# Block-causal attention with a maxout MLP on one core: transposes in two row tiles, a reordered opening, and V loaded as fp32 by SP and cast on GpSimd

## The chip, the cores and the metric

The program runs on one core of a Trainium2 chip. The metric is the device time of one execution in microseconds (us). The core has five engines with a queue each, served strictly in program order: PE (TensorE, matmuls and transposes), DVE (VectorE), ACT (ScalarE), POOL (GpSimd) and SP (SyncE, which here only issues DMAs). POOL and SP both issue DMAs, POOL's being able to change the data type on the way.

## What is computed

```python
def _attn_ref(q, k, v):                      # (8, 8, 576, 64) fp32 each
    scores = matmul(q, k.transpose(0, 1, 3, 2)) / sqrt(64)
    mask = (pos[:, None] // 64) >= (pos[None, :] // 64)     # blocks of 64
    attn = softmax(where(mask, scores, -1e9))
    return matmul(attn, v)
x = attn_out.transpose(0, 2, 1, 3).reshape(4608, 512)
g = maximum(x @ w1, x @ w2)                  # w1, w2: 512 x 1024
out = g @ w_out                              # w_out: 1024 x 512, out fp32
```

## The kernel before

The attention goes by 32 *pairs*: pair p is two heads of batch b = p // 4 (hp = p % 4 is the place of the pair in its batch). The MLP goes by 9 *spans* of 512 tokens, and its matmuls are dealt out as filler between the attention's.

Loads. `load_qk` (L84) reads q and k of a pair, each as one DMA on SP into a tile of 72 partitions (RPP = 8 rows of a head per partition). `cast_qk` (L95) turns each into bf16, on POOL for pairs 2 to 31. `load_v` (L105) reads one chunk of 128 rows of V for all 8 heads, five chunks a batch, with a DMA that POOL issues and that casts to bf16 straight into `vv` (per head 64 columns of V and one of ones). The weights come by POOL's DMAs too, 8 pieces of w1 and w2 and 2 of w_out (L117, L120). The loads after the opening stand in the list `pending` and are issued pair by pair on POOL (L331 to L335).

Opening (L124 to L139). SP issues the loads of pairs 0 to 2; POOL issues chunk 0 of V; DVE then runs constant memsets (ones column and tail of `vv`, L129 and L130, and tails of `kT` and `aT`); then the casts of pair 0 (DVE and ACT), chunks 1 to 4 of V on POOL, the casts of pair 1 on DVE, and the transposes of pair 0.

One pair (L322 to L342), in program order:

- `burst_a` (L261): scores of key chunks 0 and 1 into two PSUM tiles u0 and u1 of two banks each, both heads; the contraction has 64 rows, so the two heads use partitions 0 to 63 and 64 to 127. ACT takes the exponentials of u0 and u1 into `aT`, POOL clears the upper half of each diagonal block (`mask`, L251).
- `fill(11)`: up to 11 matmuls of the MLP.
- `burst_b` (L272): the same for chunks 2 to 4 (u2, u3), with the POOL memsets L279 and L280. u2 and u3 take the PSUM tiles of u0 and u1.
- loads and casts of later pairs.
- `av` (L283) for query tiles 0 and 1: 6 matmuls with `aT` as weights, then a reciprocal and a multiply on DVE.
- `transposes` (L218) of pair p + 1: 8 for q and 8 for k, each with 72 rows of weights and 72 columns of the identity, then a copy out of PSUM, q by DVE (L231), k by ACT (L233).
- `fill(5)`, `av` for query tiles 2, 3, 4 (24 matmuls), `fill(11)`.
- `x_out` (L308): 5 transposes of 128 x 128 and one DVE copy into `xT`, the input of the MLP.

`h_unit` (L156) has 8 matmuls of 512 columns for one eighth of w1 and w2, `y_unit` (L178) 8 for one output tile, copied out by ACT and stored by SP. `moe` (L193) yields False while the tokens of a span are not done, and `fill` then stops: during batch b there are 96 matmuls ready (64 during batch 1, none during batch 0), and they go at 27 a pair until none is left. What remains after pair 31, 224 matmuls, runs at the end. PSUM has four one-bank tiles (`ps_m`) for all but the scores.

Of the kernel before, what the change touches and what calls it, by code (L numbers as in the profile page):

```python
# [14 lines left out]
def kernel(  # L15
# [67 lines left out]

    def load_qk(p):  # L84
        b, hp = divmod(p, HP)
        raws[p] = []
        for nm, src in (("q", q), ("k", k)):
            t = raw.tile([P, 2, RPP * D], FP32, name=f"{nm}raw")
            nc.sync.dma_start(
                out=t[:NP],  # L90
                in_=src[b, 2 * hp:2 * hp + 2].rearrange("h (p t) d -> p h (t d)", t=RPP),
            )
            raws[p].append(t)

    def cast_qk(p, engines):  # L95
        qk_n[p] = []
        for nm, t, copy in zip("qk", raws.pop(p), engines):
            n = qkn.tile([P, RPP, 2, D], BF16, name=f"{nm}n")
            copy(  # L99
                out=n[:NP].rearrange("p t h d -> p h t d"),  # L100
                in_=t[:NP].rearrange("p h (t d) -> p h t d", d=D),
            )
            qk_n[p].append(n)
# [32 lines left out]
    cast_qk(0, (nc.vector.tensor_copy, nc.scalar.copy))  # L136
    for c in range(1, NCH):
        load_v(0, c)
    cast_qk(1, (nc.vector.tensor_copy, nc.vector.tensor_copy))  # L139

    def batch_loads(b):
        return [(lambda c=c: load_v(b, c)) for c in range(NCH)]

    pending = []
    for f in range(4):
        pending.append(lambda f=f: load_w(w1_sb, w1r, f * 256, 256))
        pending.append(lambda f=f: load_w(w2_sb, w2r, f * 256, 256))
    pending += batch_loads(1)
    pending += [lambda: load_wo(0, 4), lambda: load_wo(4, 4)]
    LOADS_AT = {0: 8, 1: 9}  # L150
# [42 lines left out]
    def moe():  # L193
        ny = SPAN // P
        for i in range(NSPAN):
            for f in range(NFF):
                while done_tokens[0] < (i + 1) * SPAN:
                    yield False
                for _ in h_unit(i, f):
                    yield True  # L200
# [16 lines left out]

    def transposes(p):  # L218
        b, hp = divmod(p, HP)
        tiles = []  # L220
        for nm, src in zip("qk", qk_n.pop(p)):
            pt = ps_m.tile([P, RPP, NP], BF16, name=f"ps_{nm}T", tag="m")
            for j in range(RPP):
                nc.tensor.transpose(  # L224
                    pt[:, j, :], src[:NP, j].rearrange("p h d -> p (h d)"), ident[:NP, :NP],
                )
            t = (qT_r if nm == "q" else kT_r)[p % NT]
            dst = t[:, :S].rearrange("q (p j) -> q p j", j=RPP)
            sv = pt.rearrange("q j p -> q p j")
            if nm == "q":  # L230
                nc.vector.tensor_copy(out=dst, in_=sv)  # L231
            else:
                nc.scalar.copy(out=dst, in_=sv)  # L233
# [17 lines left out]
    def mask(p, a0, n=1, step=0):  # L251
        a = aT_r[p % NA]
        if n == 1:
            nc.gpsimd.memset(a[BLK:, :, a0:a0 + BLK], 0.0)  # L254
        else:
            nc.gpsimd.memset(
                a[BLK:, :, a0:a0 + n * step].rearrange("p h (n s) -> p h n s", s=step)[:, :, :, :BLK],
                0.0,
            )
# [115 lines left out]
```

## Time and profile before

| | |
|---|---|
| median of 3 runs | 343.23 us (341.82 to 343.73) |
| the profiled execution | 338.89 us, span 337.1 us |
| PE busy | 292.4 us (87%) |
| PE weight loads busy | 157.5 us (47%) |
| DVE busy | 178.5 us (53%) |
| ACT busy | 138.8 us (41%) |
| POOL busy | 125.4 us (37%) |
| share of PE in the chain that ended last | 80% |

The profile is of one execution. Busy shares are means over stages that differ; the timeline, which lists instructions in order of time (equal neighbours merged, with their count, start and length), and the chain of waits, which is followed back from the last instruction, tell the stages apart. A matmul's length includes its way through the array, so the pace of a stream is read from start to start.

### The profile page before, as it was taken

The page shows a single profiled execution, that of the slowest core. Times are in us where ns is not written, and L with a number is a line of the kernel's source. Part 1 is how long each engine was busy: PE and PEld are TensorE (multiplying, and loading weights), DVE is VectorE, ACT ScalarE, POOL GpSimd, SP SyncE. Part 2 cuts the span into 40 slices and gives each one's busy share as a digit, 9 for nine tenths or more (in the row PEclk, how much of TensorE's full clock was granted, in tenths as well). Part 3 has the DMA queues.
Part 4 walks back from the last instruction along what each step waited for, and adds up shares of the span by engine and source line. Part 5 has one row for each costly group of instructions (what it writes and reads, how often), then busy time and mean ns, then how long its engine had stood idle before and what let it go on. Part 6 is the DMA issues. An engine that isn't in the chain of part 4 may idle for free.

```text
span 337.1 us, 7097 instructions
## 1 busy us (share of the span) xinstructions
PE 292.4 (87%) x2880; PEld 157.5 (47%) x2880; DVE 178.5 (53%) x353; ACT 138.8 (41%) x198; POOL 125.4 (37%) x244
## 2 busy tenths in 40 slices
PE   0065469996999999999999999999999998999995
PEld 0053245554555545555555555555555554444442
DVE  0242124775556655665666566656656665455440
ACT  2053434436545454545454545454554444101112
POOL 2329643554554345434543554355433300000000
PEclk9999999999999999999999999999999999999999
DMA  7899997674087559754875478548853000011013
GB/s 144 168 163 185 222 163 173 92 98 26 2 134 110 124 131 135 112 119 133 129 117 120 118 126 121 123 126 111 132 118 98 31 33 34 31 62 64 31 62 124
DMA packets 57984, 36.63 MB, mean 109 GB/s; under 512 B 39008, under 2 KB 44128, under 8 KB 57952
## 3 DMA queue, kind: packets, MB, share of 16 engines
q0 software_dynamic: 42784, 7.87, 31.5%
q1 hardware_dynamic: 15168, 28.32, 29.0%
q8 instruction: 22, 0.36, 0.5%
q14 instruction: 10, 0.08, 0.1%
HBM read 34.60 MB, written 9.44 MB: 131 GB/s over the span
## 4 chain that ended last, share of the span: by engine, by line
PE 80%; DMA 7%; issue 4%; DVE 3%; ACT 2%; POOL 2%; POOLq 0%; ACTq 0%
PE ps_h L165 37%; PE ps_y L183 18%; PE ps_o L295 10%; PE ps_s L241 7%; DMA w_sb<-in_moe_w_dram 4%; DMA vv<-in_v_dram 4%; PE ps_x L314 3%; PE ps_qT L224 2%; PE ps_kT L224 2%; ACT aT L247 2%; DVE xp L303 2%; POOL w_sb L118 1%; DVE rec L301 1%; DVE vv L130 0%; POOL qn L99 0%
## 5 line engine op out<-in xcount | busy, mean ns | idle before, releaser
L247 ACT ACTIVATE aT<-ps_s 128x1024 bf16<-128x1024 f32 (+1 forms) x128 | 99.2, 831 | 120.1 <-PE ps_s L241 119.1
L165 PE MATMUL ps_h<-xT,w_sb 128*128 128x512 bf16 x576 | 139.2, 381 | 0.0
L165 PEld LDWEIGHTS <-w_sb 128*128 128x128 bf16 x576 | 52.3, 98 | 60.7 <-issue 6.2
L172 DVE CAST h<-ps_h 128x512 bf16<-128x512 f32 x72 | 49.6, 689 | 43.9 <-PE ps_h L165 43.5
L183 PE MATMUL ps_y<-wo_sb,g 128*128 128x512 bf16 x288 | 70.6, 379 | 0.0
L174 DVE TENSOR_TENSOR g<-h,ps_h 128x512 bf16<-128x512 bf16 x72 | 49.5, 687 | 13.3 <-PE ps_h L165 12.1
L295 PE MATMUL ps_o<-vv,aT 128*128 128x65 bf16 x960 | 43.6, 200 | 7.8 <-POOL aT L254 6.9
L301 DVE RECIPROCAL rec<-ps_o 128x4 f32<-128x4 f32 x64 | 12.1, 190 | 66.8 <-PE ps_o L295 66.7
L295 PEld LDWEIGHTS <-aT 128*128 128x128 bf16 x960 | 37.8, 102 | 18.9 <-POOL aT L254 7.2
L254 POOL MEMSET aT<- 64x128 bf16 x64 | 12.7, 200 | 85.4 <-ACT aT L247 85.3
L241 PE MATMUL ps_s<-qT,kT 64*128 64x64 bf16 (+4 forms) x384 | 37.0, 296 | 6.2 <-ACT aT L247 5.5
L183 PEld LDWEIGHTS <-g 128*128 128x128 bf16 x288 | 26.9, 98 | 31.1 <-issue 1.3
L189 ACT COPY y<-ps_y 128x512 f32<-128x512 f32 x36 | 21.2, 588 | 48.0 <-PE ps_y L183 42.2
L108 POOL DMA_DIRECT2D vv<-in_v_dram x40 | 33.8, 852 | 11.8 <-DVE vv L129 11.0
L303 DVE TENSOR_TENSOR xp<-ps_o,rec 128x256 bf16<-128x256 f32 x64 | 31.4, 491 | 2.2
L99 POOL CAST qn<-qraw 72x1024 bf16<-72x1024 f32 x30 | 31.2, 1039 | 1.9
L99 POOL CAST kn<-kraw 72x1024 bf16<-72x1024 f32 x30 | 31.3, 1043 | 0.0
L224 PE MATMUL ps_qT<-ident,qn 72*128 72x72 bf16 x256 | 14.8, 205 | 18.0 <-DVE qn L99 18.0
L233 ACT COPY kT<-ps_kT 128x576 bf16<-128x576 bf16 x32 | 20.1, 628 | 22.0 <-PE ps_kT L224 21.9
L241 PEld LDWEIGHTS <-kT 64*128 64x128 bf16 x384 | 14.8, 97 | 30.6 <-issue 22.3
L279 POOL MEMSET aT<- 64x128 bf16 x32 | 6.4, 201 | 55.0 <-ACT aT L247 55.0
L314 PE MATMUL ps_x<-ident,xp 128*128 128x128 bf16 x160 | 17.4, 230 | 8.8 <-DVE xp L303 8.8
(24 smaller groups left out, 109.5 us busy)
## 6 DMA issues: line engine op xcount, KB each, us to landing
qraw<-in_q_dram SPq DMA_DIRECT2D x32, 288.0 KB
kraw<-in_k_dram SPq DMA_DIRECT2D x32, 288.0 KB
out_dram<-y SPq DMA_DIRECT2D x36, 256.0 KB
vv<-in_v_dram POOLq DMA_DIRECT2D x32, 128.0 KB, 5.8
w_sb<-in_moe_w_dram POOLq DMA_DIRECT2D x8, 256.0 KB, 8.1
wo_sb<-in_moe_w_out_dram POOLq DMA_DIRECT2D x2, 512.0 KB, 13.0
vv<-in_v_dram POOLq DMA_DIRECT2D x8, 64.0 KB, 3.3
```

The source lines that it names most:

```text
L99: copy(out=n[:NP].rearrange("p t h d -> p h t d"), in_=t[:NP].rearrange("p h (t d) -> p h t d", d=D),)
L108: nc.gpsimd.dma_start(out=vv[:rows, c, :, :D], in_=v[b, :, c * P:c * P + rows, :].rearrange("h p d -> p h d"),)
L165: nc.tensor.matmul(pt[:], w_sb[:, c, f * P:(f + 1) * P], xT[:, c, t0:t0 + SPAN], start=(c == 0), stop=(c == NDM - 1),)
L172: nc.vector.tensor_copy(out=h1[:], in_=pt[:])
L174: nc.vector.tensor_max(g[:, f, :], h1[:], pt[:])
L183: nc.tensor.matmul(py[:], g[:, f, s * P:(s + 1) * P], wo_sb[:, f, :], start=(f == 0), stop=(f == NFF - 1),)
L224: nc.tensor.transpose(pt[:, j, :], src[:NP, j].rearrange("p h d -> p (h d)"), ident[:NP, :NP],)
L241: nc.tensor.matmul(ps[:m, hh, col:col + w], kT[r, c * P:c * P + m], qT[r, q0:q0 + w], start=True, stop=True,)
L247: nc.scalar.activation(out=aT_r[p % NA][:m, :, a0:a0 + w], in_=ps[:m, :, :w], func=AF.Exp, scale=scale,)
L295: nc.tensor.matmul(po[:, gi, hh, :], a[:, hh, a0:a0 + P], vv[:, c, 2 * hp + hh, :], start=(mm == 0), stop=(mm == n_mm - 1),)
L303: nc.vector.tensor_mul(xp[:, :n], po[:, :, :, :D], rec[:, :n].to_broadcast([P, n, 2, D]))
L314: nc.tensor.transpose(pt[:, t, :], src.rearrange("p a d -> p (a d)"), ident[:])
```

## The change

- `transposes` and `x_out` work on halves of 64 partitions. q and k of a pair lie in one tile of 128 partitions (q on 0 to 63, k on 64 to 127, 9 rows of a head per partition), are cast by one instruction, and are transposed in 9 pairs of matmuls with 64 rows and 64 columns. `x_out` has 5 + 4 transposes of 64 rows into two PSUM tiles, and two copies.
- `load_v` is issued on SP into an fp32 tile `vraw` (4 buffers), and `cast_v` on POOL writes `vv`.
- The opening has another order; the weights' DMAs are all issued there, between POOL's casts; for the first four pairs both copies of the transposes and the masks are on DVE.
- The transposes of pair p + 1 go ahead of `burst_b(p)`; `x_out(p - 1)` is now the first step of pair p.
- `fill` spreads what is ready evenly over the pairs left in the batch, 2/5, 1/5 and the rest: 9, 4, 11 of 24 in batches 2 to 6; 6, 3, 7 of 16 in batch 1; 10, 5, 12 in batch 7.

```diff
-    RPP = 8
-    NP = S // RPP
+    NP = 64
+    RPP = S // NP
...
+    vraw = ctx.enter_context(tc.tile_pool(name="vraw", bufs=4))
...
     def load_qk(p):
         b, hp = divmod(p, HP)
-        raws[p] = []
-        for nm, src in (("q", q), ("k", k)):
-            t = raw.tile([P, 2, RPP * D], FP32, name=f"{nm}raw")
+        raws[p] = t = raw.tile([P, 2, RPP * D], FP32, name="raw")
+        for r, src in ((0, q), (NP, k)):
             nc.sync.dma_start(
-                out=t[:NP],
+                out=t[r:r + NP],
...
+    def cast_qk(p, copy):
+        t = raws.pop(p)
+        qk_n[p] = n = qkn.tile([P, RPP, 2, D], BF16, name="qkn")
...
     def load_v(b, c):
-        vv = vv_r[b % NV]
         rows = min(P, S - c * P)
-        nc.gpsimd.dma_start(
-            out=vv[:rows, c, :, :D],
+        v_raws[b, c] = t = vraw.tile([P, H, D], FP32, name="vraw")
+        nc.sync.dma_start(
+            out=t[:rows], in_=v[b, :, c * P:c * P + rows, :].rearrange("h p d -> p h d"),
         )
+
+    def cast_v(b, c, copy):
+        rows = min(P, S - c * P)
+        copy(out=vv_r[b % NV][:rows, c, :, :D], in_=v_raws.pop((b, c))[:rows])
...
-    for p in range(3):
-        load_qk(p)
-    load_v(0, 0)
+    dve, pool, act = nc.vector.tensor_copy, nc.gpsimd.tensor_copy, nc.scalar.copy
+    load_qk(0)
     make_identity(nc, ident)
...
+    load_v(0, 0)
+    load_qk(1)
+    load_v(0, 1)
+    load_v(0, 2)
+    load_qk(2)
+    load_v(0, 3)
+    load_qk(3)
+    load_v(0, 4)
+    cast_qk(0, dve)
+    cast_v(0, 0, pool)
+    cast_qk(1, pool)
+    cast_v(0, 1, pool)
+    load_w(0, 256)
+    cast_v(0, 2, pool)
+    load_w(256, 256)
+    cast_qk(2, pool)
+    cast_v(0, 3, pool)
+    cast_v(0, 4, pool)
+    load_w(512, 256)
+    cast_qk(3, pool)
+    load_w(768, 256)
+    load_wo(0, 4)
+    load_wo(4, 4)
...
     def transposes(p):
+        n = qk_n.pop(p)
+        pq = ps_m.tile([P, RPP, NP], BF16, name="ps_qT", tag="m")
+        pk = ps_m.tile([P, RPP, NP], BF16, name="ps_kT", tag="m")
+        for j in range(RPP):
+            for r, pt in ((0, pq), (NP, pk)):
+                nc.tensor.transpose(
+                    pt[:, j, :], n[r:r + NP, j].rearrange("p h d -> p (h d)"),
+                    ident[r:r + NP, r:r + NP],
+                )
         tiles = []
+        for pt, ring_, copy in ((pq, qT_r, dve), (pk, kT_r, dve if p < HP else act)):
...
+    def mask(p, a0):
+        eng = nc.vector if p < HP else nc.gpsimd
+        eng.memset(aT_r[p % NA][BLK:, :, a0:a0 + BLK], 0.0)
...
+        pe = ps_m.tile([P, NCH, BLK], BF16, name="ps_xe", tag="m")
+        po = ps_m.tile([P, NCH - 1, BLK], BF16, name="ps_xo", tag="m")
         for t in range(NCH):
-            nc.tensor.transpose(pt[:, t, :], src.rearrange("p a d -> p (a d)"), ident[:])
+            src = (x01[:, t] if t < 2 else x234[:, t - 2]).rearrange("p a d -> p (a d)")
+            nc.tensor.transpose(pe[:, t, :], src[:BLK], ident[:BLK, :BLK])
+            if t < NCH - 1:
+                nc.tensor.transpose(po[:, t, :], src[BLK:], ident[BLK:, BLK:])
...
     for p in range(NPAIR):
         b, hp = divmod(p, HP)
+        if p > 0:
+            x_out(p - 1)
         burst_a(p)
-        fill(11)
-        burst_b(p)
-        if p + 3 < NPAIR:
-            load_qk(p + 3)
-        if p + 2 < NPAIR:
-            cast_qk(p + 2, (nc.gpsimd.tensor_copy, nc.gpsimd.tensor_copy))
...
-        av(p, [0, 1])
+        n = -(-ready() // (HP - hp)) if p < NPAIR - HP else 27
+        fill(n * 2 // 5)
         if p + 1 < NPAIR:
             transposes(p + 1)
-        fill(5)
+        burst_b(p)
+        if p + 4 < NPAIR:
+            load_qk(p + 4)
+        if 4 <= p + 2 < NPAIR:
+            cast_qk(p + 2, pool)
+        if b + 1 < B:
+            for c in range(hp * 2, min(hp * 2 + 2, NCH)):
+                load_v(b + 1, c)
+            if hp > 0:
+                for c in range(hp * 2 - 2, min(hp * 2, NCH)):
+                    cast_v(b + 1, c, pool)
+        av(p, [0, 1])
+        fill(n // 5)
         av(p, [2, 3, 4])
-        fill(11)
-        x_out(p)
-    while next(moe_steps, None) is not None:
-        pass
+        fill(n - n * 2 // 5 - n // 5)
+    x_out(NPAIR - 1)
+    fill(len(needs))
```

## Rows read from the trace of the kernel before

**Rows 1.** The page: GB/s moved in 40 equal slices of the span.
```profile
GB/s 144 168 163 185 222 163 173 92 98 26 2 134 110 124 131 135 112 119 133 129 117 120 118 126 121 123 126 111 132 118 98 31 33 34 31 62 64 31 62 124
```

**Rows 2.** Timeline, opening: start us, length us, engine, line, operation, count [idle before, releaser].
```profile
1.27 1.02 POOL L108 DMA_DIRECT2D vv<-in_v_dram  x1 [0.81 <-POOLq L359]
...
6.18 1.04 ACT L99 CAST kn<-kraw 72x1024 bf16<-72x1024 f32 x1 [4.15 <-DMA kraw<-in_k_dram]
13.44 0.09 DVE L129 MEMSET vv<- 128x40 bf16 x1 [13.44 <-DMA vv<-in_v_dram]
...
17.35 1.22 DVE L99 CAST qn<-qraw 72x1024 bf16<-72x1024 f32 x2
...
19.90 1.03 PE L241 MATMUL ps_s<-qT,kT 64*128 64x512 bf16 x6 [0.73 <-ACT kT L233]
...
23.99 1.51 PE L295 MATMUL ps_o<-vv,aT 128*128 128x65 bf16 x24
...
25.84 5.96 POOL L118 DMA_DIRECT2D w_sb<-in_moe_w_dram  x8
...
26.82 1.04 PE L241 MATMUL ps_s<-qT,kT 64*128 64x512 bf16 x6
...
31.84 0.34 POOL L254 MEMSET aT<- 64x128 bf16 x2
```

**Rows 3.** The chain that ended last: start us, length us, engine, line, count.
```profile
54.76 0.97 PE ps_s L241 x6
55.73 3.51 PE ps_h L165 x11
...
86.09 0.54 PE ps_s L241 x6
...
251.85 0.54 PE ps_s L241 x6
...
284.82 1.79 PE ps_h L165 x8
```

**Rows 4.** Timeline of one pair in the middle, 103.3 to 112.3 us.
```profile
103.40 0.61 PE L241 MATMUL ps_s<-qT,kT 64*128 64x512 bf16 x6
...
106.42 0.42 PE L241 MATMUL ps_s<-qT,kT 64*128 64x320 bf16 x6
...
106.78 0.36 PE L295 MATMUL ps_o<-vv,aT 128*128 128x65 bf16 x6
106.92 1.18 ACT L247 ACTIVATE aT<-ps_s 128x1024 bf16<-128x1024 f32 x2
...
106.97 0.42 PE L224 MATMUL ps_qT<-ident,qn 72*128 72x72 bf16 x8
...
107.49 1.25 PE L165 MATMUL ps_h<-xT,w_sb 128*128 128x512 bf16 x5
107.73 0.75 DVE L231 COPY qT<-ps_qT 128x576 bf16<-128x576 bf16 x1
107.99 0.62 ACT L233 COPY kT<-ps_kT 128x576 bf16<-128x576 bf16 x1
108.00 0.20 POOL L279 MEMSET aT<- 64x128 bf16 x1 [1.91 <-ACT aT L247]
...
108.67 0.88 PE L295 MATMUL ps_o<-vv,aT 128*128 128x65 bf16 x24
...
109.39 2.32 PE L165 MATMUL ps_h<-xT,w_sb 128*128 128x512 bf16 x10
...
111.76 0.44 PE L314 MATMUL ps_x<-ident,xp 128*128 128x128 bf16 x5
...
112.14 0.39 PE L241 MATMUL ps_s<-qT,kT 64*128 64x512 bf16 x2
```

**Rows 5.** Timeline of PE, a batch's last pair into the next batch, 152 us.
```profile
152.00 0.34 PE L314 MATMUL ps_x<-ident,xp 128*128 128x128 bf16 x3 [0.77 <-DVE xp L303]
```

**Rows 6.** Groups by line and shape: busy us, mean ns of one | idle before.
```profile
L99 POOL CAST kn<-kraw 72x1024 bf16<-72x1024 f32 x30 | 31.3, 1043 | 0.0
```

More of the change, by code (lines that the diff above doesn't have):

```diff
@@ L73 @@
     aT_r = [ring.tile([P, 2, AW + APAD], BF16, name=f"aT{r}") for r in range(NA)]
-    xT = ring.tile([P, NDM, NTOK], BF16, name="xT")
+    xT = ring.tile([P, NDM, NTOK + BLK], BF16, name="xT")
     w1_sb = wpool.tile([P, NDM, d_ff], BF16, name="w1_sb")
@@ L85, in load_qk @@
         b, hp = divmod(p, HP)
-        raws[p] = []
-        for nm, src in (("q", q), ("k", k)):
-            t = raw.tile([P, 2, RPP * D], FP32, name=f"{nm}raw")
+        raws[p] = t = raw.tile([P, 2, RPP * D], FP32, name="raw")
+        for r, src in ((0, q), (NP, k)):
             nc.sync.dma_start(
-                out=t[:NP],
+                out=t[r:r + NP],
                 in_=src[b, 2 * hp:2 * hp + 2].rearrange("h (p t) d -> p h (t d)", t=RPP),
             )
[L93 to L103, printed above, removed]
+    def cast_qk(p, copy):
+        t = raws.pop(p)
+        qk_n[p] = n = qkn.tile([P, RPP, 2, D], BF16, name="qkn")
+        copy(
+            out=n.rearrange("p t h d -> p t h d"),
+            in_=t.rearrange("p h (t d) -> p t h d", d=D),
+        )
+    v_raws = {}
     def load_v(b, c):
-        vv = vv_r[b % NV]
         rows = min(P, S - c * P)
-        nc.gpsimd.dma_start(
-            out=vv[:rows, c, :, :D],
-            in_=v[b, :, c * P:c * P + rows, :].rearrange("h p d -> p h d"),
-        )
+        v_raws[b, c] = t = vraw.tile([P, H, D], FP32, name="vraw")
+        nc.sync.dma_start(
+            out=t[:rows], in_=v[b, :, c * P:c * P + rows, :].rearrange("h p d -> p h d"),
+        )
+    def cast_v(b, c, copy):
+        rows = min(P, S - c * P)
+        copy(out=vv_r[b % NV][:rows, c, :, :D], in_=v_raws.pop((b, c))[:rows])
     w1r = moe_w1.rearrange("(c p) f -> p c f", p=P)
@@ L115, with load_w @@
     wor = moe_w_out.rearrange("(c p) f -> p c f", p=P)
-    def load_w(dst, src, f0, fw):
-        nc.gpsimd.dma_start(out=dst[:, :, f0:f0 + fw], in_=src[:, :, f0:f0 + fw])
+    def load_w(f0, fw):
+        for dst, src in ((w1_sb, w1r), (w2_sb, w2r)):
+            nc.gpsimd.dma_start(out=dst[:, :, f0:f0 + fw], in_=src[:, :, f0:f0 + fw])
     def load_wo(c0, n):
         nc.gpsimd.dma_start(out=wo_sb[:, c0:c0 + n, :], in_=wor[:, c0:c0 + n, :])
-    for p in range(3):
-        load_qk(p)
-    load_v(0, 0)
+    dve, pool, act = nc.vector.tensor_copy, nc.gpsimd.tensor_copy, nc.scalar.copy
+    load_qk(0)
     make_identity(nc, ident)
@@ L135 @@
         nc.vector.memset(aT_r[r][:BLK, :, AW:], 0.0)
[L136 to L150, printed above, removed]
+    load_v(0, 0)
[21 more added lines that the diff above has]
+    load_wo(4, 4)
     done_tokens = [0]
@@ L195, in moe @@
         for i in range(NSPAN):
+            need = (i + 1) * SPAN
             for f in range(NFF):
[L197 to L200, printed above, removed]
+                yield from ((need, 0) for _ in h_unit(i, f))
                 if i > 0 and f % 2 == 0:
-                    for _ in y_unit(i - 1, f // 2):
-                        yield True
+                    yield from ((need, 0) for _ in y_unit(i - 1, f // 2))
@@ L204, in moe, with ready @@
         for s in range(ny):
-            for _ in y_unit(NSPAN - 1, s):
-                yield True
-    moe_steps = moe()
+            yield from ((NTOK, 0) for _ in y_unit(NSPAN - 1, s))
+    needs = []
+    for i in range(NSPAN):
+        needs += [(i + 1) * SPAN] * (2 * NDM * NFF + (SPAN // P * NFF if i else 0))
+    needs += [NTOK] * (SPAN // P * NFF)
+    moe_steps = moe()
+    at = [0]
+    def ready():
+        n = at[0]
+        while n < len(needs) and needs[n] <= done_tokens[0]:
+            n += 1
+        return n - at[0]
@@ L210, in fill @@
     def fill(n):
-        for _ in range(n):
-            if not next(moe_steps, False):
-                return
+        for _ in range(min(n, ready())):
+            next(moe_steps)
+            at[0] += 1
     st = {}
     def transposes(p):
-        b, hp = divmod(p, HP)
-        tiles = []
[L221 to L233, printed above, removed]
+        n = qk_n.pop(p)
@@ new lines, in transposes @@
+        pq = ps_m.tile([P, RPP, NP], BF16, name="ps_qT", tag="m")
[5 more added lines that the diff above has]
+                    ident[r:r + NP, r:r + NP],
+                )
+        tiles = []
+        for pt, ring_, copy in ((pq, qT_r, dve), (pk, kT_r, dve if p < HP else act)):
+            t = ring_[p % NT]
+            copy(
+                out=t[:, :S].rearrange("q (p j) -> q p j", j=RPP),
+                in_=pt.rearrange("q j p -> q p j"),
+            )
@@ L249, in exp @@
         )
[L251 to L259, printed above, removed]
+    def mask(p, a0):
+        eng = nc.vector if p < HP else nc.gpsimd
+        eng.memset(aT_r[p % NA][BLK:, :, a0:a0 + BLK], 0.0)
     def burst_a(p):
@@ L278, in burst_b @@
         exp(p, u2, 512, 1024)
-        nc.gpsimd.memset(aT_r[p % NA][BLK:, :, 1024:1088], 0.0)
-        nc.gpsimd.memset(aT_r[p % NA][BLK:, :, 1344:1408], 0.0)
+        mask(p, 1024)
+        mask(p, 1344)
         exp(p, u3, 64, 1536, m=BLK)
@@ L310, in x_out @@
         _, _, x01, x234 = st.pop(p)
-        pt = ps_m.tile([P, NCH, P], BF16, name="ps_x", tag="m")
+        pe = ps_m.tile([P, NCH, BLK], BF16, name="ps_xe", tag="m")
+        po = ps_m.tile([P, NCH - 1, BLK], BF16, name="ps_xo", tag="m")
         for t in range(NCH):
-            src = x01[:, t] if t < 2 else x234[:, t - 2]
-            nc.tensor.transpose(pt[:, t, :], src.rearrange("p a d -> p (a d)"), ident[:])
-        px = pt.rearrange("p t w -> p (t w)")[:, :S]
-        nc.vector.tensor_copy(out=xT[:, hp, b * S:(b + 1) * S], in_=px)
+            src = (x01[:, t] if t < 2 else x234[:, t - 2]).rearrange("p a d -> p (a d)")
+            nc.tensor.transpose(pe[:, t, :], src[:BLK], ident[:BLK, :BLK])
+            if t < NCH - 1:
+                nc.tensor.transpose(po[:, t, :], src[BLK:], ident[BLK:, BLK:])
+        dst = xT[:, hp, b * S:b * S + NCH * P].rearrange("p (t h w) -> p t h w", h=2, w=BLK)
+        nc.vector.tensor_copy(out=dst[:, :, 0], in_=pe[:])
+        nc.vector.tensor_copy(out=dst[:, :NCH - 1, 1], in_=po[:])
         if hp == HP - 1:
```

5 lines of the change are left out of this document (removed).

## The prediction

> **What bounds the kernel now.** I read the chain of waits first. It is PE's own work for 80%, and it falls into stages [rows 3]: batch 0 ends when pair 4's first scores start at 54.76, batch 1 at 86.09, batch 7 starts at 251.85 and the remaining 224 MLP matmuls at 284.82. From 86.09 to 251.85 are 20 pairs, 8.29 us each.
>
> One pair of the middle, from the timeline, then says what a pair costs PE [rows 4]. The 11 matmuls of a fill take 109.39 to 111.76, 0.2155 each. Both score bursts, with the changes between array shapes around them, take 0.36 (106.42 to 106.78) and 106.42 - 103.40 - 11 x 0.2155 = 0.65. The small `av` takes 0.19, the 16 transposes 0.52 (32.5 ns each), the large `av` 0.72, `x_out` with the change behind it 0.38. Ahead of the large `av` lies 0.10 (107.49 + 5 x 0.2155 = 108.57, start 108.67): it starts as the copy of kT ends (108.61), whose PSUM tile it seems to take. With the 24 matmuls that a pair has on average this sums to 8.09. A batch's last pair runs out of filler, and `x_out` waits 0.77 for DVE [rows 5], 0.19 a pair: 8.28, against 8.29 found. So the sum of rows is the stage; ACT and DVE only matter where PE waits on them.
>
> The opening is another matter [rows 2]. DVE's first memset waits until 13.44 for the first V load, because both write `vv`; DVE casts only at 17.35, and the first scores start at 19.90. Pair 0 takes 6.92 (to 26.82). Four such pairs would end at 47.6, not 54.76: the masks of pair 1, ready for ACT's results long before, sit behind 5.96 us of weight DMA issues on POOL and run at 31.84.
>
> **The change, part by part.**
>
> *Transposes.* 16 of 32.5 ns become 9 pairs. No row has tiled transposes. Lower end: the scores run two heads on the two halves, and the second burst's 2 x 576 columns fit in 0.36 with a change of shape, where one after the other they need 1152 x 0.2155 / 512 = 0.48; so the halves do overlap, and 64 columns cost 64/512 x 0.2155 = 27 ns, as `av` with 65 columns and its own weights has 30. That gives 9 x 0.03 = 0.27. Upper end: no overlap, 18 x 0.0325 = 0.59. I take 0.27, since scores are the nearest thing. `x_out` goes from 5 x 0.054 to 5 x 0.03: 0.38 becomes 0.26 (upper end 0.40). No change of shape is added, as each group now stands beside a burst. The second DVE copy lies beside the scores.
> [...]
>
> *Transposes moved ahead of burst_b.* This is what gives the gain back. ACT is served in order, so it now has the copy of kT(p + 1) ahead of the exponentials of u2. Let T be the start of the transposes. Their results are there at T + 0.45 (eight end 0.42 after their start, a ninth adds 0.03); the copy starts at T + 0.48 and takes 0.62, the next ACT instruction starts 0.1 before its end as 107.99 against 106.92 + 1.18 shows: exponentials at T + 1.0, the first mask 1.08 later (106.92 to 108.00), 0.20 long: T + 2.28 [rows 4]. PE arrives at the large `av` at T + 0.27 + 0.36 + 0.19 + 4 x 0.2155 = T + 1.68. So **a wait of 0.60 a pair** takes the place of 0.10. Ends: 0, if ACT gets to the exponentials of u2 before the copy matters (then T + 1.68 covers it); 0.9, if POOL is 0.3 late with the mask, the length of a quarter of a q-k cast ahead of it.
>
> *Middle, batches 2 to 6.* 0.26 + 0.65 + 9 x 0.2155 + 0.27 + 0.36 + 0.19 + 0.86 + 0.60 + 0.72 + 11 x 0.2155 = 8.22 a pair, with nothing left of the 0.19. Against 8.29 that is 1.4 us in 20 pairs: almost nothing.
>
> *Batch 7.* With 27 a pair the wait shrinks to 0.38 and a pair takes 8.65; the last, with 15 and an exposed multiply as before, about 7.3: 33.2 against 284.82 - 251.85 = 33.0, so +0.2. The 224 matmuls behind it and the store stay.
>
> *Batch 1.* 16 a pair: 8.22 - 8 x 0.2155 + 0.22 (a step less of cover) = 6.71, times 4 = 26.8. PE starts it at half pace: 11 matmuls took 3.51 where 2.37 is usual, and the scores 0.97 for 0.54 [rows 3], so +1.5: 28.3 against 31.3. **-3.0.**
>
> *Opening.* DVE's memsets no longer wait; they take 3.9 (13.44 to 17.35). The last of k arrived by 6.18 [rows 2]. Cast, transposes at half pace and now two DVE copies of 0.75 [rows 4]: scores of pair 0 by about 9.2. But the large `av` of pair 0 needs chunk 4 of V, the last of 13 SP loads: 8 x 0.295 + 4.5 x 0.262 = 3.54 MB. At 222 GB/s, the highest slice [rows 1], that is there at 17.2; with the 2.1 MB of weights that POOL may request before it, at 163, near 36. I take 3.54 MB at 168 from 1.3 us on, 22.4, as the weights are issued between POOL's casts, which themselves wait for these loads. POOL casts 512 columns in 0.5 (1043 ns for 1024 [rows 6]): 22.9. Then six `av` matmuls at half pace, 0.4, and 1.3 to pair 1's scores (23.99 + 1.51 to 26.82 [rows 2]): 24.6. Three more pairs: 6.92, plus at most one more copy on DVE (0.75); I take 7.2, since the masks are now on DVE and wait for no DMA issue. Pair 4 starts at 46.2 instead of 54.76: **-8.6** (ends: 38.0 with V no limit, -16.8; 59.7, +4.9).
>
> *POOL and SP.* POOL loses 40 V issues and gains 40 casts of 0.5; q and k become one cast of 1152 columns, 1.2 for 2.1. In the middle the casts end well ahead of the next pair's masks. SP gains the V loads behind `out` stores, with a pair of time to spare. Nothing, as long as V lands within a pair.
>
> Sum: -8.6 - 3.0 - 1.4 + 0.2 = -12.8. The profiled execution's 338.9 becomes 326.1. It lies 4.3 under the median of the runs, so the median 343.2 becomes **330.4 us**.
>
> **The rivals.**
>
> *A, more is gained.* V is not the limit of the opening (pair 4 at 40) and the wait is half: 330.4 - 6 - 24 x 0.3 = 317. For: the V loads' 13.44 was queueing, and SP's ring gets chunk 4 no weights ahead. Against: 3.54 MB need time.
>
> *B, the halves don't overlap.* 0.32 a pair on the transposes and 0.14 on `x_out`, 28 pairs: +12.9, 343, no change. [...]
>
> *C, slower.* Batch 1 stays at the lower clock. [...] If it doesn't rise there, batch 1's 5.9 us of PE work a pair becomes 11.8: 4 x 5.1 - 1.5 = +19, **349 us**. [...]
>
> *D, the opening's gain goes.* Chunk 4 of V arrives behind the weights, pair 4 at 59.7: 330.4 + 13.5 = 344, no change. The same comes if SP takes long over V's 1024 short runs a chunk.
>
> **How the numbers follow.** Forecast 0.50, A 0.20, B 0.13, D 0.07, C 0.10. A measurement here can tell about 0.5% (341.5 to 344.9). Forecast, A and a little of B (tiles that overlap in part) are faster: 0.76; the rest of B and D are the same: 0.13; C and a worse wait: 0.11. The range 317 to 342 leaves out A's lower half and C, and holds most of B.
>
> **What would show it.** Right: DVE's first memset before 2 us; pair 4 at 46 with pair 0's large `av` waiting for the last cast of V; 30 ns from pair to pair of tiled transposes; ACT's kT copy ahead of the u2 exponentials, and 0.6 us of PE idle ahead of L295 on POOL's mask; pairs of 8.2 in the middle. Wrong: transposes at 60 ns a pair (B), 0.43 us matmuls beyond pair 4 (C), no idle ahead of L295 (A), or pair 4 after 50 us (D).

## The result, and the profile of the changed kernel

The changed kernel takes **330.5 us** (median of 4 runs, 328.75 to 331.5) against 342.52 (4 runs, 340.61 to 343.73): ratio 0.9648, 95% interval 0.9583 to 0.9714. The forecast was 330.4. The total is right, but several of its terms are not, and that they add up to it is chance.

The page of the changed kernel: span, GB/s in 40 slices, busy time, and the chain that ended last by engine.

```profile
span 329.7 us, 7518 instructions
...
GB/s 162 213 217 200 200 212 211 184 152 67 126 161 108 123 167 166 109 117 161 171 114 82 197 164 119 103 169 162 122 42 34 34 34 33 63 35 65 32 66 127
...
PE 283.3 (86%) x3072; PEld 146.2 (44%) x3072; DVE 184.7 (56%) x403; ACT 136.4 (41%) x193; POOL 86.9 (26%) x199
...
PE 48%; issue 23%; ACT 9%; DMA 8%; POOL 6%; SPq 4%; DVE 1%; POOLq 0%; ACTq 0%; DVEq 0%
```

PE's share of the chain was 80% and is 48%; ACT went from 2 to 9%, POOL from 2 to 6%, "issue" (time in which the engine waited for nothing that the profile shows) from 4 to 23%, and SP's own issues are new in it with 4%. The first seven slices move 162 to 217 GB/s where they moved 144 to 222 [rows 1], so the opening is full of transfers in both. Where each stage starts (each pair's first scores in the timeline) tells more than the total. `before` was profiled a second time; that execution took 343.54 us, near the median, where the first took 338.89:

| stage start, us | pair 1 | pair 4 | pair 8 | pair 28 | span |
|---|---|---|---|---|---|
| before, first profile | 26.82 | 54.69 | 86.02 | 251.78 | 337.1 |
| before, second profile | 26.74 | 55.77 | 89.37 | 256.41 | 341.8 |
| after | 23.80 | 44.33 | 78.18 | 244.46 | 329.7 |

| stage, us | forecast | after less first profile | after less second profile |
|---|---|---|---|
| opening, to pair 4 | -8.6 | -10.4 | -11.4 |
| batch 1, pairs 4 to 7 | -3.0 | +2.5 | +0.3 |
| batches 2 to 6 | -1.4 | +0.5 | -0.8 |
| the rest | +0.2 | -0.1 | -0.2 |
| sum | -12.8 | -7.4 | -12.1 |

The opening gave more than forecast, batch 1 nothing. The two profiles of `before` differ by 4.7 us, 3.4 of it up to pair 8 (89.37 against 86.02) and nearly all the rest in pair 8, where none had been expected. Their windows (length, busy of PE, PEld, DVE, ACT, POOL, granted clock, DMA share, GB/s) from 76 us on, the first profile's:

```profile
76.00:90.00 14.00, 10.34 (x165) 6.42 (x164) 7.61 (x17) 7.91 (x12) 6.38 (x14) 1.00 0.27 15
```

and the second's:

```profile
76.00:90.00 14.00, 10.54 (x144) 6.88 (x142) 7.59 (x17) 7.33 (x10) 6.18 (x14) 0.83 0.46 44
```

In the second the mean granted clock of that stretch is 0.83 where the first has 1.00, 144 matmuls stand in it in place of 165, and pair 8 took 9.91 us for 8.65. Pairs 2, 4 and 7 took 1.0 to 1.2 us more as well. The sum was built on an execution without that; the 4.3 us added to reach the median allowed for it as a whole, but no term of batch 1 did.

The opening of the changed kernel (timeline, columns as in [rows 2]):

```profile
0.96 0.09 DVE L131 MEMSET vv<- 128x40 bf16 x1 [0.96 <-PEq L379]
...
6.18 1.35 DVE L97 CAST qkn<-raw 128x1152 bf16<-128x1152 f32 x1 [1.23 <-DMA raw<-in_k_dram]
...
9.77 1.04 PE L260 MATMUL ps_s<-qT,kT 64*128 64x512 bf16 x6 [1.51 <-DVE kT L249]
...
17.33 7.53 SPq L89 DMA_DIRECT2D raw<-in_q_dram  x1
...
21.66 0.61 POOL L113 CAST vv<-vraw 64x512 bf16<-64x512 f32 x1 [4.22 <-DMA vraw<-in_v_dram]
...
23.80 1.09 PE L260 MATMUL ps_s<-qT,kT 64*128 64x512 bf16 x6
```

DVE's memset starts at 0.96 instead of 13.44, and the first scores at 9.77 instead of 19.90; but pair 0's large `av` waits for the cast of V's chunk 4, which ends at 22.27, and pair 1 starts at 23.80, 3.0 us sooner and not 10. The other 7.3 us come from pairs 1 to 3, 20.5 us instead of 27.9. They are not V's: in the runs e and k below, with V by the old path and without V, pairs 1 to 3 take the same 20.5. That the masks are now on DVE and no longer behind POOL's DMA issues [rows 2] is the likely cause; it was not tried alone. One SP issue is held for 7.53 us.

A pair of the middle:

```profile
105.72 0.20 PE L242 MATMUL ps_qT<-ident,qkn 64*128 64x64 bf16 x1
105.73 0.20 PE L242 MATMUL ps_kT<-ident,qkn 64*128 64x64 bf16 x1
105.76 0.19 PE L242 MATMUL ps_qT<-ident,qkn 64*128 64x64 bf16 x1
...
105.99 0.41 PE L260 MATMUL ps_s<-qT,kT 64*128 64x320 bf16 x6
106.28 0.64 ACT L249 COPY kT<-ps_kT 128x576 bf16<-128x576 bf16 x1 [0.71 <-PE ps_kT L242]
...
106.82 1.18 ACT L266 ACTIVATE aT<-ps_s 128x1024 bf16<-128x1024 f32 x2
...
107.40 0.22 PE L308 MATMUL ps_o<-vv,aT 128*128 128x65 bf16 x2
107.90 0.34 POOL L272 MEMSET aT<- 64x128 bf16 x2 [2.08 <-ACT aT L266]
108.16 0.84 PE L308 MATMUL ps_o<-vv,aT 128*128 128x65 bf16 x22 [0.54 <-POOL aT L272]
```

The nine pairs of transposes take 0.27 (105.72 to 105.99), where 16 took 0.52 [rows 4]. ACT now copies kT before it takes the exponentials of u2 (106.28, 106.82); the mask on them follows at 107.90, and the large `av`, begun at 107.40, gets its third matmul at 108.16, where 30 ns apart is usual: some 0.70 us of wait a pair.

Batch 1's first pair, rows of POOL and of PE:

```profile
47.50 0.62 POOL L113 CAST vv<-vraw 128x512 bf16<-128x512 f32 x1 [6.02 <-DMA vraw<-in_v_dram]
48.06 1.15 POOL L97 CAST qkn<-raw 128x1152 bf16<-128x1152 f32 x1
49.26 0.20 PE L242 MATMUL ps_qT<-ident,qkn 64*128 64x64 bf16 x1 [1.44 <-POOL qkn L97]
...
50.69 0.61 POOL L113 CAST vv<-vraw 64x512 bf16<-64x512 f32 x1 [1.49 <-DMA vraw<-in_v_dram]
51.36 0.63 POOL L272 MEMSET aT<- 64x128 bf16 x4
51.61 0.51 PE L308 MATMUL ps_o<-vv,aT 128*128 128x65 bf16 x6 [1.67 <-POOL aT L272]
...
54.53 3.18 PE L175 MATMUL ps_h<-xT,w_sb 128*128 128x512 bf16 x7
```

and the same stretch in windows (columns as above):

```profile
44.00:48.00 4.00, 3.59 (x17) 1.22 (x17) 1.38 (x4) 1.94 (x2) 0.50 (x1) 1.00 1.14 225
48.00:52.00 4.00, 1.07 (x31) 0.86 (x32) 0.76 (x1) 1.72 (x3) 2.45 (x7) 0.85 1.08 221
52.00:56.00 4.00, 4.00 (x34) 2.30 (x32) 2.04 (x5) 0.00 (x0) 1.14 (x1) 0.50 1.26 204
```

POOL waits 6.02 us for a chunk of batch 1's V, casts q and k of pair 5, for whose transposes PE stands idle 1.44 us, waits 1.49 for another chunk, and only then clears pair 4's diagonal blocks; PE's `av` waits 1.67 for that. PE is busy for 1.07 of 4 us, and the granted clock is at 0.50 in the next window; seven matmuls of `h` from 54.53 on take 3.18, 0.43 apart. Pair 4 lasts 13.44 us (10.27 before; the forecast comes to 8.2).

### The profile page after: what moved, and what is told of

Read it like the earlier page. It is cut to its first block, busy times and chain, and to the rows that moved or that the text cites. A ratio compares the mean times of both kernels' runs of the same rounds, so it can differ in the third digit from the quotient of the medians.

```text
span 329.7 us, 7518 instructions
## 1 busy us (share of the span) xinstructions
PE 283.3 (86%) x3072; PEld 146.2 (44%) x3072; DVE 184.7 (56%) x403; ACT 136.4 (41%) x193; POOL 86.9 (26%) x199
## 4 chain that ended last, share of the span: by engine, by line
PE 48%; issue 23%; ACT 9%; DMA 8%; POOL 6%; SPq 4%; DVE 1%; POOLq 0%; ACTq 0%; DVEq 0%
PE ps_h L175 25%; PE ps_y L193 11%; ACT aT L266 9%; PE ps_o L308 7%; DMA vraw<-in_v_dram 5%; DMA raw<-in_k_dram 4%; SPq L89 3%; POOL aT L272 3%; PE ps_s L260 2%; PE ps_xe L328 2%; POOL qkn L97 1%; POOL w_sb L121 1%; POOL vv L113 1%; ACT y L199 0%; SPq L107 0%
## 5 line engine op out<-in xcount | busy, mean ns | idle before, releaser
L182 DVE CAST h<-ps_h 128x512 bf16<-128x512 f32 x72 | 49.7, 690 | 47.6 <-PE ps_h L175 47.4
L193 PE MATMUL ps_y<-wo_sb,g 128*128 128x512 bf16 x288 | 74.7, 379 | 0.0
L308 PE MATMUL ps_o<-vv,aT 128*128 128x65 bf16 x960 | 48.5, 201 | 26.3 <-POOL aT L272 15.5
L314 DVE RECIPROCAL rec<-ps_o 128x4 f32<-128x4 f32 x64 | 11.8, 185 | 52.8 <-PE ps_o L308 52.7
L97 POOL CAST qkn<-raw 128x1152 bf16<-128x1152 f32 x31 | 35.5, 1147 | 4.1 <-DMA raw<-in_k_dram 2.4
L113 POOL CAST vv<-vraw 128x512 bf16<-128x512 f32 (+1 forms) x40 | 23.9, 617 | 28.6 <-DMA vraw<-in_v_dram 28.5
L249 DVE COPY qT<-ps_qT 128x576 bf16<-128x576 bf16 x32 | 24.1, 752 | 5.2 <-PE ps_kT L242 4.7
L249 ACT COPY kT<-ps_kT 128x576 bf16<-128x576 bf16 x28 | 17.9, 639 | 18.6 <-PE ps_kT L242 18.3
L242 PE MATMUL ps_qT<-ident,qkn 64*128 64x64 bf16 x288 | 15.0, 199 | 9.8 <-DVE qkn L97 7.6
L260 PEld LDWEIGHTS <-kT 64*128 64x128 bf16 x384 | 17.8, 99 | 10.0 <-issue 4.2
L242 PEld LDWEIGHTS <-qkn 64*128 64x128 bf16 x576 | 11.9, 100 | 22.4 <-issue 8.1
L242 PE MATMUL ps_kT<-ident,qkn 64*128 64x64 bf16 x288 | 15.1, 199 | 0.0
```

The lines of the kernel that those rows point to most:

```text
L97: copy(out=n.rearrange("p t h d -> p t h d"), in_=t.rearrange("p h (t d) -> p t h d", d=D),)
L193: nc.tensor.matmul(py[:], g[:, f, s * P:(s + 1) * P], wo_sb[:, f, :], start=(f == 0), stop=(f == NFF - 1),)
L242: nc.tensor.transpose(pt[:, j, :], n[r:r + NP, j].rearrange("p h d -> p (h d)"), ident[r:r + NP, r:r + NP],)
L249: copy(out=t[:, :S].rearrange("q (p j) -> q p j", j=RPP), in_=pt.rearrange("q j p -> q p j"),)
L260: nc.tensor.matmul(ps[:m, hh, col:col + w], kT[r, c * P:c * P + m], qT[r, q0:q0 + w], start=True, stop=True,)
L308: nc.tensor.matmul(po[:, gi, hh, :], a[:, hh, a0:a0 + P], vv[:, c, 2 * hp + hh, :], start=(mm == 0), stop=(mm == n_mm - 1),)
```

## The experiments

Three things were open: what the middle pair's wait is, what holds pair 4, and what sets the opening. "Pair" is the mean of pairs 8 to 27, (start of pair 28 - start of pair 8) / 20; it is 8.29 before and 8.31 after.

**a_fill.** The wait, tried by more filler behind the small `av`: 7, 7, 10 for 9, 4, 11.

```diff
-        fill(n * 2 // 5)
+        n1 = (n * 3 + 5) // 10
+        fill(n1)
...
-        fill(n // 5)
+        fill(n1)
...
-        fill(n - n * 2 // 5 - n // 5)
+        fill(n - 2 * n1)
```

> The changed kernel with the filler dealt out 3/10, 3/10, 4/10 of a pair (7, 7, 10 of 24) in place of 9, 4, 11; nothing else moves. Theory (PE waits 0.7 us a pair ahead of the large av because ACT's copy of kT makes the u2 exponentials and their mask late, and only 4 matmuls cover it): with 7 the wait falls to under 0.1, a middle pair from 8.31 to about 7.67, and the whole by some 15 us, to about 315. Rival (the middle is bound by PE's own work, the tiled transposes having gained nothing): the pair stays at 8.3 and the whole at 330.

317.93 us, ratio 0.9267 (0.9207 to 0.9327), pair 7.82, short of the 7.67 expected. A pair of it:

```profile
125.84 0.38 PE L175 MATMUL ps_h<-xT,w_sb 128*128 128x512 bf16 x1
126.13 1.18 ACT L266 ACTIVATE aT<-ps_s 128x1024 bf16<-128x1024 f32 x2
126.28 1.46 PE L193 MATMUL ps_y<-wo_sb,g 128*128 128x512 bf16 x6
127.22 0.34 POOL L272 MEMSET aT<- 64x128 bf16 x2 [1.65 <-ACT aT L266]
127.57 0.88 PE L308 MATMUL ps_o<-vv,aT 128*128 128x65 bf16 x24
```

All 24 matmuls of the `av` now run through (127.57), the mask being there in time. Three more matmuls between the small and the large `av` are worth 0.49 a pair. What is left is 0.44 between a matmul of `h` and the next of `y` where 0.2155 is the pace: 0.22 that are no longer the mask's (the PSUM tile is the likely reason; that was not tried alone).

**b_kt_dve.** The same wait, by taking the copy of kT off ACT's queue.

```diff
-        for pt, ring_, copy in ((pq, qT_r, dve), (pk, kT_r, dve if p < HP else act)):
+        for pt, ring_, copy in ((pq, qT_r, dve), (pk, kT_r, dve)):
```

> The changed kernel with the copy of kT on DVE for all pairs, not for the first four alone. Theory: ACT reaches the u2 exponentials 0.33 us sooner (0.77 instead of 1.10 after the transposes' start), so the wait ahead of the large av falls from 0.70 to about 0.37, the pair from 8.31 to about 7.98, the whole by 9 us to about 321. Rival (POOL's mask is late on its own account, behind its casts): the wait stays at 0.7. A second rival: DVE, with 0.75 more a pair, gets late with the casts of h and the whole gets slower.

321.15 us, 0.9357 (0.9292 to 0.9421), pair 7.99. The large `av`:

```profile
127.04 0.22 PE L308 MATMUL ps_o<-vv,aT 128*128 128x65 bf16 x2
...
127.48 0.83 PE L308 MATMUL ps_o<-vv,aT 128*128 128x65 bf16 x22 [0.22 <-POOL aT L272]
```

With nothing of kT ahead of the exponentials the pair is 0.32 shorter, and 0.38 of the wait is left (127.10 to 127.48, at 30 ns a matmul). So the copy of kT makes a little under half of the 0.70; the rest is the way through the exponentials of u2 and their mask, which four matmuls of filler do not cover and seven do (a).

**c_late_transposes.** The transposes back behind `burst_b`, as the kernel before had them.

```diff
-        if p + 1 < NPAIR:
-            transposes(p + 1)
         burst_b(p)
...
         av(p, [0, 1])
+        if p + 1 < NPAIR:
+            transposes(p + 1)
```

> The changed kernel with the transposes of the next pair back behind the small av, where they stood before. Theory: the kT copy is again behind the u2 exponentials and the transposes cover the wait; two more changes of array shape cost about 0.2: a pair of about 7.9, the whole about 319. Rival (the tiled transposes cost more than they save once they stand alone): the pair at 8.3 or above.

319.34 us, 0.9302 (0.9227 to 0.9378), pair 7.81. Moving the transposes ahead cost 0.5 a pair, about what the tiles and the rest of the order had won.

**d_before_tiled.** In the kernel before, only the layout of q and k and the two tiled transposes, order and V as before (the diff's `load_qk`, `transposes` and `x_out`; the cast in two halves).

```diff
+        for j in range(RPP):
+            for r, pt in ((0, pq), (NP, pk)):
+                nc.tensor.transpose(
+                    pt[:, j, :], n[r:r + NP, j].rearrange("p h d -> p (h d)"),
+                    ident[r:r + NP, r:r + NP],
+                )
...
```

> The kernel before with one part of the change alone: q and k in one tile of 128 partitions, transposes and x_out in two row tiles, still two casts of a pair, the old order, V and weights as before. Theory: transposes fall from 0.52 to 0.27 plus 0.2 for two more changes of shape, x_out by 0.12: 0.17 a pair, 5 us in all, 337. Rival (tiling is all of the gain): 12 us, 330. Rival (tiles don't overlap): 343 or more.

335.77 us, 0.9791 (0.9728 to 0.9854): a gain, though not clearly one of 2%, and a time 1.2 below the expected 337. In batches 3, 5 and 6 its pairs take 8.46, 8.60, 8.60, 6.77, mean 8.11, where the kernel before has 8.28 there: 0.17 a pair, as expected. That is some 5 of the 7.3 us; at least part of the rest lies in the opening, as pair 4 starts at 53.19 for 54.69 and 55.77. In the pair at 122.47 a transpose of k starts at most 0.01 after the one of q beside it, and the ninth two start at 122.71, 0.24 after the first, in a kernel whose order did not change.

**h_q_then_k.** All of q's transposes, then all of k's, so that neighbours use the same half.

```diff
-        for j in range(RPP):
-            for r, pt in ((0, pq), (NP, pk)):
+        for r, pt in ((0, pq), (NP, pk)):
+            for j in range(RPP):
```

> The changed kernel with all 9 transposes of q ahead of all 9 of k, so that neighbours use the same half of the array. Theory (the gain of the tiles is that neighbours on different halves overlap): 18 x 0.03 = 0.54 for the transposes instead of 0.27, a pair of 8.58 instead of 8.31, the whole 7.5 us more, about 338. Rival (64 rows are cheaper by themselves, whatever the order): no change, 330.

333.74 us, 0.9725 (0.965 to 0.9799), pair 8.44: +0.13, half of the 0.27 that overlapping only between neighbours would give. PE's timeline shows why:

```profile
114.67 0.34 PE L242 MATMUL ps_qT<-ident,qkn 64*128 64x64 bf16 x6
114.83 0.20 PE L242 MATMUL ps_kT<-ident,qkn 64*128 64x64 bf16 x1
114.85 0.19 PE L242 MATMUL ps_qT<-ident,qkn 64*128 64x64 bf16 x1
...
115.00 0.31 PE L260 MATMUL ps_s<-qT,kT 64*128 64x320 bf16 x1
115.02 0.25 PE L242 MATMUL ps_kT<-ident,qkn 64*128 64x64 bf16 x3
```

Six of q's take 0.18 (114.67 to 114.85, 30 ns each, all on one half). k's first starts at 114.83, ahead of q's seventh at 114.85; from there q's and k's take turns to 114.93, and the first score matmul starts at 115.00, ahead of the last three of k's at 115.02. So the order strictly by program that is said above of all five queues is not that of PE's rows here.

**e_v_by_pool.** V as before, by POOL's casting DMA, all else as after.

```diff
-        nc.sync.dma_start(
-            out=t[:rows], in_=v[b, :, c * P:c * P + rows, :].rearrange("h p d -> p h d"),
+        nc.gpsimd.dma_start(
+            out=vv_r[b % NV][:rows, c, :, :D],
+            in_=v[b, :, c * P:c * P + rows, :].rearrange("h p d -> p h d"),
...
```

> The changed kernel with V loaded as before, by POOL's casting DMA straight into vv, at the places where the change has the load on SP; no cast of V. Theory (V on SP's queue, in turn with q and k, is what brings pair 1 forward; POOL's V loads land late beside SP's, at 16.7 to 28.6 us where they were issued by 6): pair 1 starts near 30 instead of 23.8; pair 4 itself gets shorter, as no mask waits behind a cast of V; the whole within 3 us of 330, 332. Rival (V on SP with its 256-byte runs is a loss): faster than 327.

331.68 us, 0.9732 (0.9671 to 0.9794), no difference from the changed kernel (`after`) that these runs can tell. But the stages differ: pair 1 at 28.90 (after 23.80), pair 4 lasts 8.72 (after 13.44), and pairs 1 to 3 take 20.5 in both. The new path of V gains 5.1 us in the opening and loses 4.7 in pair 4.

**f_pool_queue.** The masks of pairs 4 and 5, and the casts of q and k for pairs 4 to 6, from POOL to DVE.

```diff
-        eng = nc.vector if p < HP else nc.gpsimd
+        eng = nc.vector if p < HP + 2 else nc.gpsimd
...
-            cast_qk(p + 2, pool)
+            cast_qk(p + 2, dve if p + 2 < HP + 3 else pool)
```

> The changed kernel with the masks of pairs 4 and 5 and the casts of q and k of pairs 4 to 6 on DVE, out of POOL's queue, where they stand behind casts of V that wait for their loads. Theory (pair 4 takes 13.4 us instead of about 8 because POOL's queue is held by V of batch 1, PE stands idle 3 us and its clock falls again): pair 4 takes about 9.3, the whole 4 us less, about 326. Rival (pair 4 is long because PE runs at the lower clock at its start whatever POOL does): pair 4 stays over 12.

327.86 us, 0.9567 (0.9492 to 0.9641). Pair 4 lasts 9.65 and not 13.44; pairs 2 and 3 are 0.4 longer each, with the casts on DVE. The masks, and the cast of q and k of pair 5, waited in POOL's queue, behind casts that waited for V.

**g_wo_later.** The two DMAs of w_out from the end of the opening to pairs 4 and 5.

```diff
-    load_wo(0, 4)
-    load_wo(4, 4)
...
+        if p in (4, 5):
+            load_wo((p - 4) * 4, 4)
```

> The changed kernel with the two loads of w_out issued in pairs 4 and 5 instead of in the opening. Theory (the V loads of batch 1 are late because SP's DMA issues are held for up to 7.5 us while the weights share the DMA engines): 2 MB less between 26 and 47 us lets chunks 2 to 4 of batch 1 land 3 to 6 us sooner, pair 4 takes about 10, the whole 3 us less, about 327. Rival (the short runs of V alone hold SP): no change, 330.

326.15 us, 0.9511 (0.9449 to 0.9574); pair 4 lasts 8.41, less than the 10 expected. POOL's last two casts of batch 1's V, and PE's window from 48 us:

```profile
41.54 0.62 POOL L113 CAST vv<-vraw 128x512 bf16<-128x512 f32 x1 [0.90 <-DMA vraw<-in_v_dram]
...
44.92 0.61 POOL L113 CAST vv<-vraw 64x512 bf16<-64x512 f32 x1 [1.67 <-DMA vraw<-in_v_dram]
```

```profile
48.00:52.00 4.00, 3.24 (x45) 1.85 (x40) 3.04 (x7) 1.68 (x3) 2.18 (x4) 1.00 1.09 203
```

They ran at 47.50 and 50.69 in after: V comes 6 us sooner when w_out's 2 MB do not share the transfers. SP's issues are held nearly as long as before (7.08, 5.45 and 4.50 us for 7.53, 5.57 and 4.64), so what w_out cost V lies in the transfers and not in these holds. PE has 45 matmuls in the window where it had 31, and the clock stays at 1.00.

**i_before_memsets.** In the kernel before, chunk 0 of V issued behind the memsets, so that nothing makes DVE wait.

```diff
-    load_v(0, 0)
     make_identity(nc, ident)
...
-    for c in range(1, NCH):
+    for c in range(NCH):
         load_v(0, c)
```

> The kernel before with one edit: the first load of V is issued after DVE's constant memsets, which then wait for no DMA. Theory (the wait of the memsets delays the whole opening): first scores near 9 instead of 19.9 and pair 4 about 10 us sooner, the whole about 333. Rival (the opening is bound by POOL's queue and by the loads behind it anyway): pair 4 starts less than 3 us sooner, the whole above 340.

My theory fell: 341.03 us (10 runs, 336.8 to 343.44); the ratio, over five of them from 336.8 to 339.7, is 0.9874 (0.9827 to 0.9921), within the 2% that count as the same; and pair 4 starts at 54.21 for 54.69. PE in its opening:

```profile
10.13 1.04 PE L240 MATMUL ps_s<-qT,kT 64*128 64x512 bf16 x6 [2.88 <-DVE qT L230]
16.70 0.32 PE L294 MATMUL ps_o<-vv,aT 128*128 128x65 bf16 x3 [3.70 <-DMA vv<-in_v_dram]
...
25.22 0.32 PE L294 MATMUL ps_o<-vv,aT 128*128 128x65 bf16 x3 [8.20 <-DMA vv<-in_v_dram]
...
31.19 1.03 PE L240 MATMUL ps_s<-qT,kT 64*128 64x512 bf16 x6
```

The scores do start at 10.13, ten us sooner, and then PE waits 3.70 and 8.20 us for V itself: issued on POOL by 5.92 us, its chunks land from 16.7 us on, beside SP's loads of q and k. Removing the wait showed the next one. So the changed kernel's opening is not won by the memsets alone.

**k_no_v.** The bound of everything about V: the kernel leaves out V's loads and casts, and its result is not the attention's.

```diff
     def load_v(b, c):
+        return
     def cast_v(b, c, copy):
+        return
...
```

> The changed kernel without V: no load and no cast of V, vv set to 0.5 by POOL at the start (the loads of V and their casts are left out). Theory (chunk 4 of V, last of the loads on SP, sets pair 1's start, and V's loads hold SP's issues and POOL's queue in pair 4): pair 1 starts near 17 instead of 23.8, pair 4 takes about 8.3 instead of 13.4, SP has no issue held over 2 us, the whole about 318. Rival (q, k and the weights alone keep the DMA engines as busy): pair 1 at 22 or later and SP still held.

319.38 us, 0.9373 (0.9317 to 0.9429). Pair 1 starts at 16.26 (after 23.80), pair 4 lasts 8.40 (13.44): 7.5 + 5.0 us, against the 12.3 by which its span (317.4) is shorter. V's path costs the changed kernel nothing else that these stages show. The issue on SP that took 7.53 us, q of pair 5,

```profile
10.38 0.59 SPq L88 DMA_DIRECT2D raw<-in_q_dram  x1
```

takes 0.59, and none up to 62 us takes over 0.71 (two later ones, at 74 and 166 us, take 1.80 and 2.15).

**j_split_and_wo.** The version that should beat both: g, and a split of 6, 8, 10 of 24 (5, 5, 6 of 16; 7, 9, 11 of 27).

```diff
-        fill(n * 2 // 5)
+        n1 = (n + 1) // 4 + (n < 20)
+        n2 = n // 3
+        fill(n1)
...
-        fill(n // 5)
+        fill(n2)
...
-        fill(n - n * 2 // 5 - n // 5)
+        fill(n - n1 - n2)
...
```

> The changed kernel with w_out loaded in pairs 4 and 5, and the filler dealt out 6, 8, 10 of 24 (5, 5, 6 of 16; 7, 9, 11 of 27). Theory: the wait ahead of the large av is covered; besides, with 7, 7, 10 PE waited 0.22 a pair for the copy of qT, whose PSUM tile the next y tile takes, and one matmul of h more behind the transposes covers that too: a middle pair of 7.6, pair 4 about 8, the whole about 309. Rival (the second burst, now earlier, waits for ACT to free the PSUM tiles of the first): a pair of 7.8 or more.

**311.69 us**, 0.9147 (0.9081 to 0.9214), pair 7.72, pair 4 8.07.

```profile
128.56 0.59 PE L172 MATMUL ps_h<-xT,w_sb 128*128 128x512 bf16 x2
...
128.99 1.46 PE L190 MATMUL ps_y<-wo_sb,g 128*128 128x512 bf16 x6
129.84 0.34 POOL L269 MEMSET aT<- 64x128 bf16 x2 [1.44 <-ACT aT L263]
130.29 0.90 PE L305 MATMUL ps_o<-vv,aT 128*128 128x65 bf16 x24
```

The first `y` follows the two `h` at the usual pace (0.43 for two), and the mask is done at 130.18, just before the `av`: neither the 0.70 nor the 0.22 is left. The pair is 0.1 above the 7.6 expected and the whole 2.7 above the 309; two of the 20 pairs take 8.00 and 7.98, and in the second of these PE waits for ACT inside the second burst (166.96), as the rival had it.

## Why the prediction was right, and where it was wrong

- **The tiles: right.** 0.27 for nine pairs, 30 ns a pair, as forecast, and in d alone -0.17 a pair. Rival B is out. In h, six transposes in a row on the same half took 30 ns each (114.67 to 114.85), each with its own weights.
- **The wait that replaces a wait: right, 0.70 for 0.60.** Copy of kT at T + 0.56 (forecast 0.48), exponentials at T + 1.10 (1.0), the waiting matmul at T + 2.44 (2.28), with T = 105.72. That is the 0.09 between a pair of 8.31 and the forecast's 8.22. The forecast said of this step that it gives the gain back, and a, b and c, which shrink the wait in three ways, each get 0.3 to 0.5 a pair. Its cause, the copy of kT ahead of the exponentials, is 0.32 of the 0.70 (b); that PE comes to the `av` with only four matmuls of filler ahead is the rest.
- **POOL's casts: right in the middle.** 1.15 for q and k (forecast 1.2), 0.62 for 512 columns of V (0.5), with the groups by line of the changed kernel's page standing beside [rows 6]:

```profile
L97 POOL CAST qkn<-raw 128x1152 bf16<-128x1152 f32 x31 | 35.5, 1147 | 4.1 <-DMA raw<-in_k_dram 2.4
...
L113 POOL CAST vv<-vraw 128x512 bf16<-128x512 f32 (+1 forms) x40 | 23.9, 617 | 28.6 <-DMA vraw<-in_v_dram 28.5
```

The last column points at what went wrong: POOL stood 28.5 us ahead of `cast_v`, waiting for V. All of it lies before 51 us, and the 6.02 and 1.49 ahead of pair 4's masks are the part that cost batch 1.
- **The opening: right in its limit, 1.9 us too slow.** V's chunk 4 was cast by 22.27 (22.9 forecast), the first scores came at 9.77 (9.2), pair 1 at 23.80 (24.6), and pairs 1 to 3 took 6.90, 6.90 and 6.73 (7.2). That V sets pair 1's start, which rival A denied, k shows. 1.1 of the 1.9 us are the three pairs that were put at 7.2 each.
- **Batch 1: wrong by 5.5 us.** "POOL and SP" was put at "Nothing, as long as V lands within a pair", and batch 1 at **-3.0**; it came out at +2.5. V did not land within a pair. SP's issues were held (7.53, and while pairs 1 to 3 ran 5.57, 4.64, 3.43 us), the last weights shared the transfers, which g shows to be what counted, and POOL, served in order, stood at `cast_v` with the cast for pair 5 and the masks of pair 4 behind it. The forecast looked at the queue in the middle, where it was right, and not at the stage where all of it comes together. Its pairs 5 to 7 (6.80 each) fit the 6.71 forecast; nearly the whole miss is pair 4, 13.44 for 8.2 (8.41 in g). This is what rival D named, V arriving behind the weights, but one batch later.
- **Rival C: in part.** Matmuls of `h` go from 0.43 to full pace at about 47.4, and back to 0.43 in pair 4 (granted clock 0.50 from 52 to 56), after PE had stood idle 1.44 and 1.67 us behind POOL; but full pace is back as pair 5 starts (57.77: six score matmuls in 0.62, where pair 4's took 1.09). No run shows the 11.8 of the sum, a pair of batch 1 wholly at half pace: pairs 5 to 7 take 6.80 each. What makes the clock rise is not shown either. From 51.61 to 57.64 PE works without a gap at half pace; at full pace that is about 3.0 us less (an estimate, half of those 6.03), the larger part of the 5.0 by which pair 4 exceeds g's 8.41. f and g show that POOL's queue sets it off: there pair 4 takes 9.65 and 8.41, and `h` keeps its full pace from 49.7 and 48.5 on. The mean clock of the other executions of `after` (1.000 with 331.0 us, 0.999 with 328.75, 0.994 with 329.98) cannot tell what pair 4 cost in them: a's profile has a stretch at half pace (five matmuls of `h` in 2.33 us) under a column of 1.00:

```profile
52.00:56.00 4.00, 3.94 (x33) 2.36 (x33) 1.84 (x5) 0.00 (x0) 0.91 (x1) 1.00 1.26 206
...
51.65 2.33 PE L175 MATMUL ps_h<-xT,w_sb 128*128 128x512 bf16 x5
```

- **The total: right by chance.** The terms were built on the first profile of `before`. Against it the opening gave 1.8 more than forecast, batch 1 5.5 less, the middle 1.9 less and the rest 0.3 more: 7.4 us for 12.8. The missing 5.4 were made up by the 4.3 that the forecast added to reach the median of `before`, and by the profiled execution of `after` lying 1.0 above its own median. No term says that the changed kernel pays those 4.3, and in the second profile of `before` they lie in pairs 2, 4, 7 and 8. Against that profile the opening gave 2.8 more and batch 1 3.3 less, with middle and rest within 0.6 each: there too the total is right because misses cancel.

Open: what holds an issue on SP for up to 7.5 us. It goes with V's loads on SP (k, e). Weights beside them are not needed: in `after` an issue at 5.91 us is held 3.81, and POOL's first weight DMA is issued at 11.99. V's loads are not enough by themselves: two of them at 112.05 take 1.21 us together. Whether the number of short runs matters was not tried. That the PSUM tile makes the 0.22 in a is argued from the rows only, and what the masks on DVE gave pairs 1 to 3 was not tried alone.

## What to carry to other kernels

Before work is moved to a queue that is served in order, look at the stage where the most transfers meet, not only at the steady state: here a cast on POOL that waited 6.02 us for a DMA held another cast and the masks behind it, and moving two weight loads was worth 4.4 us, a third of what the whole change brought. When a reordering puts a copy ahead of the work that the next consumer needs, rebalance the filler around the new wait at once; three matmuls of 24 were worth 0.49 us a pair. And profile the kernel before twice: an execution 4 us under its median hid stages that vary.
